# Who issues the stores of the block sums in the first mixing stage: SyncE one step later, or GpSimd right behind its additions

## The chip, the core and the metric

The kernel runs on one core of a Trainium2 chip. The core has a matrix engine (TensorE, PE in the profile) and three engines for elementwise work: VectorE (DVE), ScalarE (ACT) and GpSimd (POOL). SyncE (SP) does no arithmetic in this kernel; it issues most of the DMA transfers. ScalarE and GpSimd issue a few. Each engine takes its instructions in the order in which the program lists them, and waits on semaphores for the others.

The metric is the device time of one execution in microseconds (us). Before the change the median of three runs is 1366.9 us (1365.86 to 1368.06).

## What is computed

Two layers of the same form follow each other on 2048 tokens of width 512, all in float32. Each layer is a linear-attention block and then a gated MLP whose gate mixes the tokens:

```python
x = x + A(layernorm(x))                                   # linear attention, 32 heads
def B(x):                                                 # gated MLP with token mixing
    z  = gelu(x @ w_in)                                   # 2048 x 1792
    z1, z2 = z[:, :896], layernorm(z[:, 896:])
    g  = w_sp @ z2 + b_sp[:, None]                        # w_sp is 2048 x 2048: the mixing
    return (z1 * g) @ w_out
x = x + B(layernorm(x))
```

`w_sp` and the other weights are the same in both layers.

## The kernel before

**Precision.** A float32 product is made of three matmuls: each operand is split into a high part (ScalarE, a copy to float32r) and the remainder (VectorE, a subtraction), and high times high, high times low and low times high are added in the accumulators. In the mixing stage these three are lines 1619, 1620 and 1621.

**The mixing.** The product `w_sp @ z2` is taken with a block algorithm of Strassen's kind, which needs sums of blocks of `w_sp` as operands. The four sums of a block column are made once, in layer one, by class `Sums`, written to the DRAM tensors `s[m, k]` (m from 1 to 4, k from 0 to 7), and read back as operands in both layers. Class `P4` is the mixing. In layer one its order is eight steps each of the products P4, P1, P6, P7, P5 and P3, and then fourteen steps of a nested product N2: steps 0 to 61. A step of P4, P1 or P5 has 24 matmuls, one of P6, P7 or P3 has 18, and one of N2 has 12.

**One step `g` of `P4.run`**, in program order: `prepare(g + 2, g + 3)` splits the weights of step g + 2 (ScalarE line 1457, VectorE line 1466) and the activations of step g + 3 (ScalarE line 1462; VectorE line 1470 or 1472); `mm(g)` issues the matmuls; `fetch(g + 4)` has SyncE load the raw weights of step g + 4 into a `qd` tile (line 1413 from `w_sp`, line 1415 from the sums `s`, 512 KB each), which waits until TensorE has released such a tile; `sums.tick(g, MIX_TICKS)` is the place of the change; then come the steps of `own` (an `Inner` object, which makes the operands of N2: loads on line 1263, ScalarE and VectorE work on lines 135, 138 and 1299 to 1306, stores on line 1267), and `gates` (GpSimd lines 1639 and 1641, from step 24 on). Behind the last step of a product `evac` has VectorE add the accumulators to the result; behind P6 that is line 1669, and P7 goes on in the same accumulators, so its first matmul into each of them waits for that read.

**The sums.** `MIX_TICKS` lists the 26 steps on which block sums are made: 2, 4, 5, 7, 8, 10, 12, 14, 16 and 17 make three sums each (m = 1, 3 and 2, in this order), and the sixteen from step 20 to step 41 make one each (m = 4). SyncE loads the blocks one step ahead (`fetch`, line 1195 for the first kind, line 131 for the second), GpSimd adds (line 1209), and line 1202 stores each sum of 128 x 512 (256 KB). That is 10 x 3 + 16 = 46 stores. Another 18 are made earlier, in the token stage, by `P2.run`, which calls `sums.store()` and `sums.sum()` itself. P6 uses the sums with m = 2: its last step, 23, reads the sums that step 17 makes for k = 7, and their load is issued by `fetch(23)` in step 19.

**Pages.** Buffers of 128 x 512 are named `pg` and come from a list of 23. A page that is given back can be handed out again after six more requests (`lag=STORE`); whoever gets it waits until its last readers are done, a store's landing among them.

Of the kernel before, what the change touches and what calls it, by code (L numbers as in the profile page):

```python
# [90 lines left out]
def mixer_kernel(ctx: ExitStack, tc: tile.TileContext, x_in, wqkv, wo_d, win1_d, win2_d, wsp_d, bsp_d, wout_d,  # L91
                 ident_d, mask_d, out_d):
    nc = tc.nc
# [109 lines left out]
    class Make:  # L203
# [22 lines left out]
        def store(self, g):  # L226
            m = 2 * len(self.raw[g])
            h, l, p = self.part.pop(g)
            for n, t in enumerate((h, l)):
                nc.sync.dma_start(kept[:, m:m + 2, g, n, :], t.rearrange("p (m f) -> p m f", m=2))  # L230
            pages.put(p, l, lag=STORE)
# [942 lines left out]
    class Sums:  # L1174
# [21 lines left out]
                    raw.append(t)  # L1196
                self.raw.append(raw)

        def store(self):

            for m, k, j, t, done in self.made:
                nc.sync.dma_start(self.s[m, k][:, j, :], t)
                for t in (t, *done):
                    if id(t) in pages.held:
                        pages.put(t, lag=STORE)
            self.made = []
# [4 lines left out]

        def tick(self, i, at):

            self.store()
            if i + 1 in at:
                self.fetch()
            self.sum(i, at)

        def sum(self, i, at):

            if i not in at:
                return
            k, j, fourth = self.todo.popleft()
            if fourth:
                s2, a12 = self.raw.popleft()
                self.add(4, k, j, a12, s2, a12, s2)
            else:
                a21, a22, a11 = self.raw.popleft()
                self.add(1, k, j, a22, a21, a22)
                self.add(3, k, j, a21, a21, a11)  # L1230
                self.add(2, k, j, a11, a22, a11)
# [687 lines left out]
```

## Time and profile before

| | |
|---|---|
| median of three runs | 1366.9 us (1365.86 to 1368.06) |
| the profiled execution | 1367.67 us, of which 1366.0 us lie between the first and the last instruction |
| TensorE | busy 1355.8 us, 99% of the span |
| VectorE | busy 1030.4 us (75%) |
| ScalarE | busy 638.2 us (47%) |
| GpSimd | busy 475.8 us (35%) |
| mean granted TensorE clock | 0.997 |

The profile is one execution. In its rows a DMA issue stands under the engine that issues it, with a q for the queue (SPq, POOLq), and its length is the issue alone; the transfer lands later. `qd<-s` is a load of block sums into a quad, `s<-pg` the store of a sum from a page, `bg` the result of the mixing. A row "xN" merges N equal instructions that follow each other. The mixing stage of layer one lies between 344.6 us and some 615 us.

### The profile page before, as it was taken

The page shows a single profiled execution, that of the slowest core. Times are in us where ns is not written, and L with a number is a line of the kernel's source. Part 1 is how long each engine was busy: PE and PEld are TensorE (multiplying, and loading weights), DVE is VectorE, ACT ScalarE, POOL GpSimd, SP SyncE. Part 2 cuts the span into 40 slices and gives each one's busy share as a digit, 9 for nine tenths or more (in the row PEclk, how much of TensorE's full clock was granted, in tenths as well). Part 3 has the DMA queues.
Part 4 walks back from the last instruction along what each step waited for, and adds up shares of the span by engine and source line. Part 5 has one row for each costly group of instructions (what it writes and reads, how often), then busy time and mean ns, then how long its engine had stood idle before and what let it go on. Part 6 is the DMA issues. An engine that isn't in the chain of part 4 may idle for free.

```text
span 1366.0 us, 18322 instructions
## 1 busy us (share of the span) xinstructions
PE 1355.8 (99%) x6087; PEld 1134.7 (83%) x6087; DVE 1030.4 (75%) x1582; ACT 638.2 (47%) x1021; POOL 475.8 (35%) x551
## 2 busy tenths in 40 slices
PE   9999999999999899999999999999999999999998
PEld 7888888888888788888888888888888888888887
DVE  7985898876856788986678768887767798978642
ACT  6875553445443343442456655444455534533310
POOL 2333475533254237426421133533230011412340
PEclk9999999999999999999999999999999999999999
DMA  5762488966798888795786534666568798569652
GB/s 185 240 207 88 123 262 260 311 224 189 227 338 307 286 268 284 276 374 184 222 261 195 193 95 123 201 210 205 187 200 283 220 338 322 189 200 311 222 183 90
DMA packets 184496, 310.18 MB, mean 227 GB/s; under 512 B 15696, under 2 KB 67920, under 8 KB 180304
## 3 DMA queue, kind: packets, MB, share of 16 engines
q1 hardware_dynamic: 172736, 262.73, 58.3%
q0 software_dynamic: 8064, 39.85, 8.2%
q10 hardware_dynamic: 3600, 6.42, 1.3%
q8 instruction: 48, 0.79, 0.2%
q14 instruction: 48, 0.39, 0.1%
HBM read 211.68 MB, written 97.26 MB: 226 GB/s over the span
## 4 chain that ended last, share of the span: by engine, by line
PE 94%; DVE 3%; ACT 1%; issue 1%; DMA 1%; POOL 0%; DVEq 0%; ACTq 0%; POOLq 0%
PE bank L151 17%; PE bank L149 17%; PE bank L150 17%; PE bank L1619 9%; PE bank L1620 9%; PE bank L1621 9%; PE bank L1552 4%; PE bank L1553 4%; PE bank L1550 4%; PE bank L994 1%; PE bank L995 1%; PE bank L993 1%; PE bank L736 1%; DMA qd<-s 1%; DVE pg L138 0%
## 5 line engine op out<-in xcount | busy, mean ns | idle before, releaser
L1619 PE MATMUL bank<-qd,pg 128*128 128x512 f32 x544 | 213.1, 392 | 3.6 <-DVE bg L1669 3.6
L1620 PE MATMUL bank<-qd,pg 128*128 128x512 f32 x544 | 213.0, 392 | 0.0
L1621 PE MATMUL bank<-qd,pg 128*128 128x512 f32 x544 | 212.8, 391 | 0.0
L1466 DVE TENSOR_TENSOR qd<-qd,qd 128x1024 fp32r<-128x1024 f32 x104 | 144.2, 1387 | 78.0 <-ACT qd L1457 77.5
L1457 ACT ACTIVATE qd<-qd 128x1024 fp32r<-128x1024 f32 x104 | 110.0, 1058 | 144.6 <-DMA qd<-s 53.3
L151 PE MATMUL bank<-qd,pg 128*128 128x512 f32 x380 | 148.7, 391 | 0.3 <-DVE pg L138 0.3
L135 ACT ACTIVATE pg<-pg 128x512 fp32r<-128x512 f32 (+1 forms) x146 | 89.3, 620 | 117.4 <-DVE pg L330 43.8
L268 POOL TENSOR_SCALAR rs<-mv 128x1 f32<-128x1 f32 x95 | 42.2, 444 | 264.8 <-DVE mv L266 260.3
L1641 POOL TENSOR_TENSOR bg<-bg,pg 128x512 f32<-128x512 f32 x56 | 93.0, 1672 | 104.7 <-DMA pg<-z 93.2
L1209 POOL TENSOR_TENSOR pg<-pg,pg 128x512 f32<-128x512 f32 x52 | 81.8, 1574 | 133.3 <-DMA pg<-in_wsp_dram 121.2
L1619 PEld LDWEIGHTS bank<-qd,pg 128*128 128x128 f32 x544 | 102.8, 189 | 25.4 <-ACT qd L1457 4.0
L1620 PEld LDWEIGHTS bank<-qd,pg 128*128 128x128 f32 x544 | 102.9, 189 | 21.4
L1621 PEld LDWEIGHTS bank<-qd,pg 128*128 128x128 f32 x544 | 102.9, 189 | 21.4
L138 DVE TENSOR_TENSOR pg<-pg,pg 128x512 fp32r<-128x512 f32 (+1 forms) x143 | 107.4, 751 | 14.8 <-ACT pg L135 14.0
L149 PE MATMUL bank<-qd,pg 128*128 128x512 f32 x284 | 111.0, 391 | 0.0
L150 PE MATMUL bank<-qd,pg 128*128 128x512 f32 x284 | 110.7, 390 | 0.0
L149 PE MATMUL bank<-bg,qd 128*128 128x448 f32 x256 | 94.1, 368 | 0.0
L150 PE MATMUL bank<-bg,qd 128*128 128x448 f32 x256 | 93.7, 366 | 0.0
L330 DVE STREAM_TRANSPOSE pg<-pg 128x512 f32<-128x512 f32 x79 | 86.1, 1090 | 10.0 <-DMA pg<-yt 8.4
L151 PE MATMUL bank<-bg,qd 128*128 128x448 f32 x256 | 93.5, 365 | 0.0
L1552 PE MATMUL bank<-qd,pg 128*128 128x512 f32 x224 | 87.4, 390 | 0.3 <-DVE qd L1466 0.3
L1550 PE MATMUL bank<-qd,pg 128*128 128x512 f32 x224 | 87.2, 389 | 0.0
(220 smaller groups left out, 3192.4 us busy)
## 6 DMA issues: line engine op xcount, KB each, us to landing
qd<-s SPq DMA_DIRECT2D x64, 512.0 KB, 4.2
qd<-n POOLq DMA_DIRECT2D x32, 1024.0 KB, 7.8
pg<-in_wsp_dram SPq DMA_DIRECT2D x93, 256.0 KB, 4.7
qd<-in_wsp_dram SPq DMA_DIRECT2D x40, 512.0 KB, 5.2
s<-pg SPq DMA_DIRECT2D x58, 256.0 KB, 4.9
pg<-z SPq DMA_DIRECT2D x56, 256.0 KB, 3.9
n<-pg SPq DMA_DIRECT2D x55, 256.0 KB, 4.5
x<-pg SPq DMA_DIRECT2D x48, 256.0 KB, 2.7
```

The lines of the kernel that those rows point to most:

```text
L138: nc.vector.tensor_sub(l, src, h.bitcast(F32))
L149: nc.tensor.matmul(out, ah, bh, start=start, stop=False)
L150: nc.tensor.matmul(out, ah, bl, start=False, stop=False)
L151: nc.tensor.matmul(out, al, bh, start=False, stop=stop)
L1457: nc.scalar.activation(wh, r, AF.Copy)
L1466: nc.vector.tensor_sub(wl, r, wh.bitcast(F32))
L1550: m(out[i], h[:, o, f], w[:, o, 0], start=first and name in ("P1", "P2", "P5"), stop=False, skip_group_check=True)
L1552: m(out[i], h[:, o, f], w[:, o, 1], start=False, stop=False, skip_group_check=True)
L1619: m(out, h[:, o], w[:, 0, j, :], start=start, stop=False, skip_group_check=True)
L1620: m(out, h[:, o], w[:, 1, j, :], start=False, stop=False, skip_group_check=True)
L1621: m(out, l[:, o], w[:, 0, j, :], start=False, stop=stop, skip_group_check=True)
L1641: nc.gpsimd.tensor_tensor(u, u, z1, op=OP.mult)
```

## The change

The stores of the mixing stage are issued on GpSimd's queue instead of SyncE's. `tick` calls `store` at its end, behind this step's additions, where it called it at its beginning, for the additions of the step before. The pages are therefore also given back earlier in program order. The stores of the token stage stay on SyncE, a step later.

```diff
-        def store(self):
+        def store(self, issue=nc.sync):
 
             for m, k, j, t, done in self.made:
-                nc.sync.dma_start(self.s[m, k][:, j, :], t)
+                issue.dma_start(self.s[m, k][:, j, :], t)
                 for t in (t, *done):
                     if id(t) in pages.held:
                         pages.put(t, lag=STORE)
...
         def tick(self, i, at):
 
-            self.store()
             if i + 1 in at:
                 self.fetch()
             self.sum(i, at)
+            self.store(nc.gpsimd)
```

In the program that results, GpSimd has 46 more DMA issues, each group of three behind its three additions, and SyncE has 46 fewer. The arithmetic instructions of every engine are the same and in the same order.

## Prediction

> **What bounds the kernel now.** I read the page first, for the engine that fills the span and the groups with idle time before them.
>
> ```profile
> span 1366.0 us, 18322 instructions
> PE 1355.8 (99%) x6087; PEld 1134.7 (83%) x6087; DVE 1030.4 (75%) x1582; ACT 638.2 (47%) x1021; POOL 475.8 (35%) x551
> L1619 PE MATMUL bank<-qd,pg 128*128 128x512 f32 x544 | 213.1, 392 | 3.6 <-DVE bg L1669 3.6
> ```
>
> TensorE is busy for 99% of the span, so only its gaps can be won. The largest that the mixing shows is one of 3.6 us, ended by VectorE's line 1669, the read of the accumulators behind P6. The timeline of TensorE there:
>
> ```profile
> 431.67 0.39 PE L1619 MATMUL bank<-qd,pg 128*128 128x512 f32 x1
> ...
> 464.08 0.39 PE L1621 MATMUL bank<-qd,pg 128*128 128x512 f32 x1
> 468.06 0.76 PE L1619 MATMUL bank<-qd,pg 128*128 128x512 f32 x1 [3.59 <-DVE bg L1669]
> ...
> 475.10 0.39 PE L1619 MATMUL bank<-qd,pg 128*128 128x512 f32 x1
> ```
>
> The first row opens step 16 (P6 begins), the second is the last matmul of step 23, the third opens step 24, the last opens step 25. Eight steps of 18 matmuls run at one start per 0.227 us: (464.08 - 431.67) / 143. Step 24 should open at 464.31 and opens at 468.06: 3.75 us late. It should last 18 x 0.227 = 4.08 us and lasts 475.10 - 468.06 = 7.04: another 2.96 us. The table by windows says why (columns: TensorE, its weight loads, VectorE, ScalarE, GpSimd busy, granted clock, DMA share, GB/s):
>
> ```profile
> 460.00:465.00 5.00, 4.47 (x20) 3.38 (x18) 3.74 (x5) 1.87 (x4) 2.15 (x1) 1.00 0.81 262
> 465.00:470.00 5.00, 1.94 (x5) 1.58 (x6) 4.97 (x8) 1.33 (x2) 1.21 (x1) 0.74 1.02 321
> 470.00:475.00 5.00, 5.00 (x15) 3.92 (x14) 4.82 (x7) 1.99 (x3) 1.46 (x2) 0.58 0.97 353
> ```
>
> The granted clock is 1.00 before the gap, 0.74 and 0.58 behind it. The place costs 3.75 + 2.96 = 6.71 us, 0.49% of the span. The chain of waits leads back from it:
>
> ```profile
> 451.71 6.86 DMA qd<-s
> 458.68 1.07 ACT qd L1457
> ...
> 467.23 0.70 DVE bg L1669
> 468.06 0.76 PE bank L1619
> ```
>
> VectorE reaches line 1669 at 467.23 because a load of block sums, issued by SyncE at 451.71, landed only at 458.57, and the splits of that load and of what followed it stand ahead of line 1669 in VectorE's order: 467.23 - 458.57 = 8.66 us. Why was the load late? The timeline of SyncE and its waits between 344 and 475 us:
>
> ```profile
> 415.55 0.73 SPq L1415 DMA_DIRECT2D qd<-s  x1
> 420.59 1.58 SPq L1195 DMA_DIRECT2D pg<-in_wsp_dram  x3
> 422.28 4.47 SPq L1415 DMA_DIRECT2D qd<-s  x2
> 428.00 3.41 SPq L1202 DMA_DIRECT2D s<-pg  x3
> 431.46 1.39 SPq L1195 DMA_DIRECT2D pg<-in_wsp_dram  x3
> 432.96 0.36 SPq L1415 DMA_DIRECT2D qd<-s  x1
> 433.43 2.94 SPq L1195 DMA_DIRECT2D pg<-in_wsp_dram  x3
> ...
> 443.83 3.92 SPq L1202 DMA_DIRECT2D s<-pg  x3
> 450.34 0.32 SPq L1415 DMA_DIRECT2D qd<-s  x1
> ```
>
> ```profile
> SPq L1202 <- POOL pg L1209: 38.7, 27, 4.7
> SPq L1415 <- DMA s<-pg: 2.5, 1, 2.5
> ```
>
> Waiting at its stores (line 1202) for GpSimd's additions is by far SyncE's longest wait here, 38.7 us in 27 waits, and every load stands behind it. In the last rows of the timeline it issues the three stores of step 17 as the additions end, until 447.75; then the weights of step 23, which are one of those very sums, wait 2.5 us for the store to land, until 450.34; the load of the chain follows at 451.71.
>
> **The change part by part.** *SyncE loses 46 stores.* An issue is short (the merged 38.7 us are waiting), so what counts is the loads that move up, and they are still held by TensorE, which frees their tiles. The loads for step 16's sums stood behind step 14's stores, at 431.46; now they follow the weight load that ends at 422.28 + 4.47 = 426.75, 4.7 us sooner. Those for step 17 stood at 433.43; the weight load ahead of them waits for step 15's end, 431.67, so they go out at 432.1, 1.3 us sooner.
>
> *GpSimd gains 46 issues.* No store on its queue is in this trace; the nearest rows are its loads. The first pair is 256 KB each, the second 1 MB.
>
> ```profile
> L975 POOL DMA_DIRECT2D pg<-win_sums x24: 535/557/765, 310.3 to 1013.5; - x24
> DMA to landing us min/median/max: 3.0/4.4/6.8
> ...
> L1403 POOL DMA_DIRECT2D qd<-n x32: 527/528/596, 580.3 to 1267.7; - x32
> DMA to landing us min/median/max: 5.1/7.8/11.4
> ```
>
> An issue is 0.557 us of GpSimd's time (0.53 to 0.77), in all 46 x 0.557 = 25.6 us. What is queued behind them is the next additions, from step 24 on the gates, and from 580.3 us N2's weight loads (line 1403). The first are covered by GpSimd's own idle time:
>
> ```profile
> 426.44 4.62 POOL L1209 TENSOR_TENSOR pg<-pg,pg 128x512 f32<-128x512 f32 x3 [6.25 <-DMA pg<-in_wsp_dram]
> 436.87 10.54 POOL L1209 TENSOR_TENSOR pg<-pg,pg 128x512 f32<-128x512 f32 x6 [5.81 <-DVE qd L1466]
> ```
>
> It idles 6.25 and 5.81 us before these groups; three issues take 1.67 us. Only steps 16 and 17 follow each other without a pause (six additions in 10.54 us). If the cover is gone, their 1.67 us delay the sums of step 17, and that is in the sum below.
>
> *The path.* Step 16's additions began 436.87 - 431.46 = 5.4 us behind the first of their loads; now 426.8 + 5.4 = 432.2, and 4.62 us for three ends them at 436.8, their stores at 438.5. Step 17's loads, out at 432.1, are there at 437.5 by the same 5.4, so its additions run from 438.5 to 443.1. Their last store, m = 2, is the one that step 23 needs: it stands behind two others and starts at 443.1 + 1.1 = 444.2. Its landing takes 3.0 to 11.4 us by the rows; I take 4.4, the median for this size, so 448.6. Step 23's load can leave then instead of at 450.34: 1.7 us sooner, with bounds of 3.1 sooner (447.2) and 5.3 later (455.6).
>
> The Trainium skill prices this leg too: its page DMA: Bandwidth & Descriptors, section Anatomy of one DMA, fits 2.0 us plus bytes over 436e3 for the software path, which for 256 KB is an estimate of 2.6 us, so a landing at 446.8, 3.5 us sooner than now, and a gap of 0.2 us; the rows of this trace, 3.0 at the least, do not reach that figure.
>
> *A new wait.* The pages of step 17's loads are now those that step 14's stores release on GpSimd's queue, and SyncE would stand at them. Step 14's loads move up from 420.59 to 416.3, behind the row at 415.55, its additions began 426.44 - 420.59 = 5.85 us behind them and take 4.62, so they end at 426.8, and the third store lands at 426.8 + 1.1 + 4.4 = 432.3: 0.2 us behind the 432.1 at which SyncE wants the page. I cost it at nothing, since GpSimd is busy with step 16 until 438.5.
>
> *The sum.* With everything from step 23's load on 1.7 us sooner, line 1669 starts at 465.5 and the gap is 3.75 - 1.7 = 2.05 us. Its other end is zero: the load of the chain took 6.86 us to land, and the median of its kind is 4.2.
>
> ```profile
> qd<-s SPq DMA_DIRECT2D x64, 512.0 KB, 4.2
> ```
>
> At that latency another 2.7 us go, and VectorE is in time. The 2.96 us at the low clock came behind a gap of 3.59 us; whether a gap of 2.05 brings them no row here shows. The bounds are that they stay (gain 1.7) or go (4.66); I take that they go, as the gap is little over half as long. So the gain is 4.66 to 6.71, I take the middle, 5.7, and 1367.67 - 5.7 = 1362.0 for the profiled execution, which lies 0.77 above the median of the runs: 1361.2 for the median.
>
> The page TensorE: Matmul & The Clock Gate, Part 1 (The HAM clock gate), says that the clock halves after an idle window of about 3.4 us. The drop behind 3.59 us agrees; by that rule 2.05 us would leave the clock alone and the gain is at least 4.66, and by a rule under which any gap drops it, 1.7.
>
> What is late next? Step 25's weights, issued at 453.70 before (its tile is free at the start of step 21, 452.07), so again 1.6 us sooner; from step 26 on the fetches have caught up with TensorE. Behind step 24 I see no gap that this would open.
>
> **The rivals.** *No gain:* the last store lands as late as the 6.8 us of the longest 256 KB row, at 451.0, 0.7 us later than now, or the gap shrinks but keeps the low clock. This gives 1366.9 + 0.7 = 1367.6 to 1366.9 - 1.7 = 1365.2. For it: two stores now stand ahead of the one that matters, where SyncE had issued them while GpSimd was still adding. Against it: step 16's loads win 4.7 us.
>
> *Slower:* the software queue is the bound. The last store of step 17 lands only after the 11.4 us of that queue's longest row, at 455.6. Step 23's load then leaves 5.3 us later, the gap grows from 3.75 to 9.0 us, the low clock stays: 1366.9 + 5.3 = 1372.2. It decides from a landing of 8.8 us on (444.2 + 8.8 = 453.0, 2.7 later). For it: the 1 MB loads have a median of 7.8, and GpSimd's addition stretches from 1276 to 2370 ns in the company of VectorE, so its descriptor writing might.
>
> ```profile
> L1209 POOL TENSOR_TENSOR pg<-pg,pg x52: 1276/1525/2370, 182.1 to 554.7; 128x512 f32<-128x512 f32 x52
> ```
>
> Against it: a store is a quarter of such a load, and the issues of both groups keep to 0.53 to 0.77 us. The Trainium skill's DMA page, section SWDGE vs HWDGE vs iDMA, names the mechanism: the software path writes its descriptors through SBUF, where VectorE can lock GpSimd out, and SyncE's path is immune.
>
> **How the numbers follow.** A measurement of this kernel tells about 0.2% (2.7 us) from no change. The forecast (gap shrunk or gone, clock kept: 1360.2 to 1362.2) has 0.62, no gain 0.20, slower 0.18. Faster by over 0.2% is the forecast alone, 0.62; within 0.2% 0.20; slower 0.18. The range runs from 1359.2, the full 6.71 with another 1 us for the spread of the runs, to 1368.6, the end of "no gain" with the same 1 us; left out is the slower case.
>
> **What would show it.** In the profile after, the gap before line 1619 from line 1669 should be 2 us or none and the granted clock 1.00 from 460 to 475; SyncE's wait for line 1209 should be gone; the loads for step 16's sums should go out near 427, the weights of step 23 before 450; GpSimd's line 1202 should show 46 issues of some 0.56 us with landings near 4.4. A landing over 8.8 us, a new gap behind another product, or a gap of 3.6 that stays would prove me wrong.

## The result, and the profile after

The changed kernel is slower by a little: 1368.8 us median (1365.6 to 1371.4, 21 runs) against 1365.9 (1363.1 to 1368.5, 21 runs) for the kernel before; ratio 1.0021, 95% interval 1.0013 to 1.0029. The profiled execution took 1368.05 us. The forecast was 1361.2.

The page after, the lines that answer to those of the page before:

```profile
span 1366.3 us, 18345 instructions
PE 1354.5 (99%) x6087; PEld 1133.1 (83%) x6087; DVE 1037.8 (76%) x1582; ACT 638.4 (47%) x1021; POOL 500.9 (37%) x597
L1619 PE MATMUL bank<-qd,pg 128*128 128x512 f32 x544 | 212.2, 390 | 4.8 <-DVE bg L1669 4.8
```

GpSimd took the 25 us of issues that were expected (475.8 to 500.9). But TensorE's pause before line 1619 is still there, ended by the same line 1669, and it is 4.8 us instead of 3.6. TensorE's timeline and the table by windows (columns as before):

```profile
464.20 0.39 PE L1621 MATMUL bank<-qd,pg 128*128 128x512 f32 x1
469.38 0.53 PE L1619 MATMUL bank<-qd,pg 128*128 128x512 f32 x1 [4.79 <-DVE bg L1669]
...
475.13 0.39 PE L1619 MATMUL bank<-qd,pg 128*128 128x512 f32 x1
```

```profile
465.00:470.00 5.00, 0.62 (x2) 0.59 (x3) 3.76 (x6) 2.65 (x4) 1.82 (x2) 0.96 0.88 320
470.00:475.00 5.00, 5.00 (x17) 3.94 (x17) 4.81 (x9) 1.67 (x3) 1.83 (x2) 0.69 0.90 299
```

By the arithmetic of the prediction, step 24 opens 469.38 - 464.20 - 0.23 = 4.95 us late, and lasts 475.13 - 469.38 - 4.08 = 1.67 us too long at the low clock. The place costs 6.62 us, where it cost 6.71: the gap is 1.20 us longer, and the low clock behind it costs 1.29 us less. No view ties the second to the change, so it counts as luck. The two profiled executions are accordingly nearly equal; the medians are 3 us apart.

Was SyncE freed? Its timeline and its waits from 344 to 475 us:

```profile
426.96 1.33 SPq L1195 DMA_DIRECT2D pg<-in_wsp_dram  x3
431.98 0.33 SPq L1415 DMA_DIRECT2D qd<-s  x1
433.99 1.76 SPq L1195 DMA_DIRECT2D pg<-in_wsp_dram  x3
...
436.79 12.83 SPq L1415 DMA_DIRECT2D qd<-s  x3
...
450.69 0.36 SPq L1415 DMA_DIRECT2D qd<-s  x1
```

```profile
SPq L1415 <- DMA s<-pg: 8.7, 1, 8.7
SPq L131 <- DMA s<-pg: 5.3, 1, 5.3
```

The wait of 38.7 us at line 1202 is gone, the loads for step 16's sums go out at 426.96, and the load of the chain, step 24's, goes out at 450.69 instead of 451.71. But one wait at line 1415 grew from 2.5 to 8.7 us: SyncE now stands at the load of step 23's weights, the last of the three merged into the row at 436.79, for the landing of the sum that step 17 makes, and issues it at 449.3. (The 5.3 us at line 131 end with a load at 467.09, too late to bear on this pause.)

What holds line 1669, then? The chain of waits leads elsewhere than before:

```profile
445.73 3.45 DMA s<-pg
...
450.21 5.18 DMA pg<-in_wsp_dram
...
455.56 1.60 POOL pg L1209
...
457.45 6.99 DMA s<-pg
...
464.48 0.04 issue
464.52 0.04 ACTq L135
464.56 0.05 issue
464.60 0.04 ACT pg L135
...
465.14 1.05 ACT qd L1457
...
468.55 0.69 DVE bg L1669
```

ScalarE's line 135 (a split for `Inner`, in step 22) wants a page, and the page is still being read by the store of step 20's sum, which GpSimd issued at 457.45 and which landed 6.99 us later. The split of step 25's weights (line 1457) stands behind line 135 on ScalarE, VectorE's subtraction behind that, and line 1669 behind both. Further back the chain leads to the same landing at which SyncE stood: the blocks of step 20's sum are loaded behind step 23's weights (450.21), so the sum is added at 455.56 and stored at 457.45. The view of line 1202 names everyone who waited for such a store (its landings are those of all 64 stores of that line; the 46 on GpSimd's queue alone landed in 2.7, 5.7 and 8.0 us):

```profile
L1202 POOL DMA_DIRECT2D s<-pg x46: 539/557/583, 361.0 to 555.2; - x46
...
who waited for it (us, times):
  ACT pg L135: 5.9, 1
...
DMA to landing us min/median/max: 2.7/5.6/8.0
```

In the profile before, the same instruction of line 135 waited for VectorE only, and began at 463.28 (ScalarE's waits from 440 to 470 us, and the chain of waits); here it began at 464.60, though step 24's weights had come earlier:

```profile
ACT pg L135 <- DVE pg L1306: 3.1, 1, 3.1
```

```profile
463.28 0.40 ACT pg L135
```

The pages are given back where `store` is called. With the call at the end of the tick, each page is back a step earlier in program order, and so it is handed out to another user: line 135 drew a page that a store was still reading.

### The profile page after: what moved, and what is told of

It is laid out like the page before. It is cut to its first block, busy times and chain, and to the rows that moved or that the text cites. A ratio compares the mean times of both kernels' runs of the same rounds, so it can differ in the third digit from the quotient of the medians.

```text
span 1366.3 us, 18345 instructions
## 1 busy us (share of the span) xinstructions
PE 1354.5 (99%) x6087; PEld 1133.1 (83%) x6087; DVE 1037.8 (76%) x1582; ACT 638.4 (47%) x1021; POOL 500.9 (37%) x597
## 4 chain that ended last, share of the span: by engine, by line
PE 87%; DVE 4%; DMA 3%; ACT 2%; POOL 2%; issue 1%; SPq 0%; DVEq 0%; POOLq 0%; ACTq 0%
PE bank L151 16%; PE bank L149 16%; PE bank L150 16%; PE bank L1619 8%; PE bank L1620 8%; PE bank L1621 8%; PE bank L1552 4%; PE bank L1553 4%; PE bank L1550 4%; PE bank L995 1%; PE bank L994 1%; PE bank L993 1%; DMA s<-pg 1%; POOL pg L1209 1%; DMA pg<-in_wsp_dram 1%
## 5 line engine op out<-in xcount | busy, mean ns | idle before, releaser
L1621 PE MATMUL bank<-qd,pg 128*128 128x512 f32 x544 | 212.3, 390 | 0.0
L138 DVE TENSOR_TENSOR pg<-pg,pg 128x512 fp32r<-128x512 f32 (+1 forms) x143 | 110.6, 774 | 15.0 <-ACT pg L135 13.8
L1209 POOL TENSOR_TENSOR pg<-pg,pg 128x512 f32<-128x512 f32 x52 | 85.2, 1639 | 100.2 <-DMA pg<-in_wsp_dram 80.4
L1621 PEld LDWEIGHTS bank<-qd,pg 128*128 128x128 f32 x544 | 102.6, 189 | 21.2
L330 DVE STREAM_TRANSPOSE pg<-pg 128x512 f32<-128x512 f32 x79 | 86.1, 1090 | 10.7 <-DMA pg<-yt 8.5
```

Source lines behind the costliest of these rows:

```text
L138: nc.vector.tensor_sub(l, src, h.bitcast(F32))
L1209: nc.gpsimd.tensor_tensor(t, a, b, op=OP.add)
L1621: m(out, l[:, o], w[:, 0, j, :], start=False, stop=stop, skip_group_check=True)
```

## The experiments

The runs form three groups, each timed on one chip beside the kernel before: the first four; the reverse with the sixteen changed and the three with earlier sums; and the three runs that stand between these. The theories at first: theory 1, the pages (line 135 draws a page that a store is still reading); theory 2, the queue (stores on GpSimd cost something by themselves); a third, the place (the earlier call costs on either queue). Those of the later runs are named in their expectations. In kernels with two more lines, L1417, L1621 and L1671 are the lines 1415, 1619 and 1669 of the others.

**GpSimd's queue alone, at the old place.** The pages are handed out as in the kernel before.

```diff
         def tick(self, i, at):
 
-            self.store()
+            self.store(nc.gpsimd)
```

> The stores go out on GpSimd's queue, but at the old place, at the beginning of the next step, so that every page goes to the same holder as before the change. Theory 1 (pages): the changed kernel loses because the store at the end of the step gives its page back earlier in program order, and ScalarE's line 135 of step 22 takes that page and waits for the landing of step 20's store at 464.44 us. Then line 135 starts near 461.5 here, right behind line 1306, line 1669 follows 3.95 us later as in the kernel before, near 465.4, the gap before step 24 is 2 us or none and the clock stays at 1.00: about 1361 to 1363 us, a ratio to the kernel before of about 0.998. Theory 2 (queue): stores on the software queue cost by themselves, wherever the pages go (0.56 us of GpSimd each, landings of 5.6 us in the median against 4.9): the gap of some 4 to 5 us stays, about 1368 to 1369 us, a ratio of 1.002.

Measured: 1367.9 us (11 runs) against 1365.3 (21 runs), ratio 1.0018 (1.0009 to 1.0027). Line 135 waits for no store of a sum, and the pause is shorter in the profile, though not the 2 us or none of theory 1:

```profile
PE bank L1619 <- DVE bg L1669: 2.4, 1, 2.4
```

The clock falls behind it, the time is within 0.1 us of theory 2's range, and the ratio hardly below the changed kernel's 1.0021. So the pages are not the whole cause.

**The earlier place alone, on SyncE.**

```diff
         def tick(self, i, at):
 
-            self.store()
             if i + 1 in at:
                 self.fetch()
             self.sum(i, at)
+            self.store()
```

> The stores stay on SyncE, but are issued at the end of the step behind its additions, so that the pages go to the same holders as in the changed kernel. Theory 1: ScalarE's line 135 waits for step 20's store here too, but on SyncE that store lands some 3.4 us behind its issue (459.06 to 462.45 in the kernel before), which is before line 135 could start (463.28): no loss by the page, and SyncE still waits for GpSimd at every store: within 0.1% of the kernel before. Theory 2: as the kernel before as well. A third theory, that the earlier place costs on either queue, gives 1.002.

Measured: 1379.1 us (4 runs), ratio 1.0104 (1.009 to 1.0117), which none of the three theories foresaw. SyncE now waits for the additions of its own step, and a new pause of 10.7 us opens at the start of P6 (some 431 us):

```profile
SPq L1202 <- POOL pg L1209: 59.5, 28, 6.5
```

```profile
PE bank L1619 <- DVE bg L1666: 10.7, 1, 10.7
```

The two halves of the change belong together: the earlier place needs the other queue. Since SyncE itself is later here, the run does not tell what the pages cost.

**The changed kernel with a longer lag** (twelve page requests instead of six before a page of a store is used again).

```diff
-            self.store(nc.gpsimd)
+            self.store(nc.gpsimd, 2 * STORE)
```

> The changed kernel, but a page given back by these stores is handed out again only after 12 requests and not after 6. Theory 1: line 135 of step 22 gets a page that no fresh store holds, so the gap before step 24 is 2 us or none: 1361 to 1363 us, a ratio of about 0.998, if no other instruction gets a worse page. Theory 2: 1368 to 1369 us, a ratio of 1.002.

Measured: 1369.4 us (5 runs), ratio 1.0037 (1.0024 to 1.0051). Line 135's wait for a store is gone, the pause is 3.3 us, and another of 1.1 us stands at some 546 us. The time is 0.4 us above the range of theory 2 and far from that of theory 1; but the longer lag holds back every page of the 46 stores, out of 23 pages in all, so this run does more than take away that one wait.

**Thirty stores changed, sixteen left.** The ten steps with three sums store on GpSimd at the step's end; the sixteen with one sum (from step 20 on) store on SyncE a step later.

```diff
         def tick(self, i, at):
 
+            self.store()
             if i + 1 in at:
                 self.fetch()
             self.sum(i, at)
-            self.store(nc.gpsimd)
+            if self.made and self.made[0][0] != 4:
+                self.store(nc.gpsimd)
```

> The thirty stores of the ten steps that make three sums go out on GpSimd as in the changed kernel; the sixteen of the steps that make one sum stay on SyncE a step later, as before the change. Theory 1: the store of step 20, whose page line 135 waited for, is among the sixteen, so the wait is gone: gap of 2 us or none, 1361 to 1363 us, a ratio of about 0.998. Theory 2: thirty of 46 stores still cost, a ratio of 1.001.

Measured: 1365.0 us (11 runs), ratio 0.9996 (0.9988 to 1.0005): the loss is gone, with no gain in its place; neither forecast is met. The profile still has a pause:

```profile
PE bank L1621 <- DVE bg L1671: 2.6, 1, 2.6
```

**The reverse: sixteen changed, thirty left.** The condition reads `== 4`.

> The reverse of the run with the thirty stores of three-sum steps on GpSimd: here those thirty stay on SyncE a step later, as before, and the sixteen stores of the one-sum steps (from step 20 on) are issued by GpSimd right behind their additions, as changed. Theory S (the loss sits in the sixteen: their pages are given back one step sooner in program order, and their landings from GpSimd's queue come late): 1367.0 to 1369.5 us, with ScalarE's line 135 waiting several us for such a store's landing at some 457 to 464 us. Theory T (the loss needs the thirty as well): 1365.3 us within 0.8, gap before line 1619 about 3 us as before.

Measured: 1370.6 us (5 runs) against 1366.2 (26 runs), ratio 1.0035 (1.0022 to 1.0049), 1.1 us above the range of theory S. ScalarE's and TensorE's waits show what theory S describes (the store went out at 459.89 and landed at 466.36):

```profile
ACT pg L135 <- DMA s<-pg: 5.3, 1, 5.3
```

```profile
PE bank L1621 <- DVE bg L1671: 6.1, 1, 6.1
```

The loss sits in the sixteen stores from step 20 on, which the prediction did not look at.

**The sixteen on GpSimd's queue at the old place**, the thirty on SyncE. Against the kernel before:

```diff
-            self.store()
+            self.store(nc.gpsimd if self.made and self.made[0][0] == 4 else nc.sync)
```

> As the run with only the sixteen one-sum stores on GpSimd, but at the old place (a step later in program order), so that the pages are handed out as before; the thirty others stay on SyncE. Theory P: line 135 no longer waits for a landing of a sum's store; of the 4.4 us which the sixteen cost with the pages given back sooner, 3 us or more go: 1365.5 to 1367.5 us. Rival (the sixteen on GpSimd's queue cost it by themselves, whatever the pages): 1369 to 1371 us.

**The changed kernel and GpSimd's queue alone, once more,** beside the last run:

> The changed kernel once more, for a second profile and for its time beside the two others of this call. Theory P (the page that ScalarE's line 135 of step 22 waits for, from the store of step 20's sum): the wait at line 135 shows again with 3 to 6 us, the pause before line 1619 at some 464 us is 4 us or more, and the time is 1 us or more above the kernel with GpSimd's queue at the old place. Theory O (the second place, the end of P5 at some 542 us, where GpSimd's additions slow VectorE down): a second pause at line 1678 of 1 us or more shows too.

> All stores on GpSimd's queue, at the old place (a step later in program order, so that the pages are handed out as before), a second time, for a second profile. Theory P: no wait of line 135 for a landing of a sum's store; the time is 0.5 to 1.5 us below the changed kernel's and so 2 to 3 us above before. Where those 2 to 3 us lie is open: theory O puts them at line 1678 (some 542 us, a pause of 1 us or more); theory C (GpSimd's addition of step 21 runs beside VectorE's line 138 ahead of line 1669 and stretches it from 0.69 to 1.78 us) puts them at line 1669, with a pause of 3 us or more and the low clock behind it.

Measured, against 1365.8 us (29 runs): the changed kernel 1368.65 (12 runs), ratio 1.0019 (1.0009 to 1.003); the queue alone 1367.0 (12 runs), 1.0007 (0.9994 to 1.0021); the sixteen at the old place 1367.7 (11 runs), 1.0015 (1.0006 to 1.0025), a little above what theory P gave. In the second profile of the changed kernel the wait for the page shows again, 7.0 us, with a pause of 5.7:

```profile
ACT pg L135 <- DMA s<-pg: 7.0, 1, 7.0
```

```profile
PE bank L1619 <- DVE bg L1669: 5.7, 1, 5.7
```

The other two have no such wait. Keeping the pages as before is worth 1368.65 - 1367.0 = 1.6 us here, and, for the sixteen alone, the ratio falls from 1.0035 to 1.0015, which is 2.7 us, across two groups of runs. From the first result to the first run of the queue alone it falls by 0.4 us only (1.0021 to 1.0018). The intervals of these pairs overlap, so that the pages cost something is likely, and how much is not settled. The sixteen at the old place have a long pause without any wait for a page:

```profile
PE bank L1619 <- DVE bg L1669: 4.3, 1, 4.3
```

The pause at 542 us that theory O expected shows in none of the three profiles; theory O falls as their cause. What remains above before is 1.2 to 2.6 us, the 1.2 of this group within its noise. For it the profiles show one candidate, theory C. VectorE ahead of line 1669 with GpSimd's queue alone, and GpSimd at the same time:

```profile
463.70 0.55 DVE L1470 TENSOR_TENSOR pg<-pg,pg 128x384 fp32r<-128x384 f32 x1
464.29 1.71 DVE L138 TENSOR_TENSOR pg<-pg,pg 128x512 fp32r<-128x512 f32 x1
465.92 2.47 DVE L1669 TENSOR_TENSOR bg<-bank,pg 128x512 f32<-128x512 f32 x4
```

```profile
464.18 1.27 POOL L1209 TENSOR_TENSOR pg<-pg,pg 128x512 f32<-128x512 f32 x1 [3.51 <-PE bank L1621]
```

Line 138 takes 1.71 us beside this addition of GpSimd's, the third of the single ones and so that of step 23 (the expectation has step 21); without company it takes 0.69, and there the addition comes later. The kernel with thirty stores changed:

```profile
465.69 0.69 DVE L138 TENSOR_TENSOR pg<-pg,pg 128x512 fp32r<-128x512 f32 x1
```

```profile
466.98 1.29 POOL L1209 TENSOR_TENSOR pg<-pg,pg 128x512 f32<-128x512 f32 x1 [5.77 <-DVE bg L1671]
```

In the first run of the queue alone line 138 takes 1.78 us, and with the sixteen at the old place line 1470 takes 1.62 where it takes 0.55. That is 1.0 to 1.1 us on the path in each. It was not tried by itself: no run moved that addition and nothing else. The pause in the profiles of the queue alone is only 2.1 and 2.4 us, against the 3 that theory C asked for and the 3.6 of the kernel before, and these two executions are 1.3 and 1.7 us below the medians of their kernels. So theory C is argued, not shown, and what the 1.2 to 2.6 us hold stays open.

**Step 17's sums a step earlier.** If SyncE's long wait for that landing starts the pause, making those sums earlier ends it. The same edit on three kernels: on the one with thirty stores on GpSimd, on the kernel before, and on the changed kernel.

```diff
-MIX_TICKS = (2, 4, 5, 7, 8, 10, 12, 14, 16, 17, 20, ...
+MIX_TICKS = (2, 4, 5, 7, 8, 10, 12, 13, 15, 16, 20, ...
```

> Thirty stores on GpSimd at the step's end, sixteen on SyncE a step later, and the last three of the three-sum steps one step earlier (13, 15 and 16 in place of 14, 16 and 17). Theory B (the pause between P6 and P7 starts with SyncE standing at the load of step 23, for the landing of step 17's third sum, with the loads of steps 24 and 25 queued behind it): that load goes out at about 444.3 instead of 449.25, step 24's at about 448.4 instead of 450.6 and lands at 454 to 455; VectorE's line 1669 comes 8.6 us behind that, at 463 to 464 instead of 466.3; pause under 0.5 us, no low clock: 1359.5 to 1361.5 us. Rival Q (other waits of the stage, such as pages for line 135 or VectorE's order, set line 1669 anyway): pause of 2 us or more and 1364 to 1366 us.

> The kernel before with the last three of the three-sum steps one step earlier (13, 15 and 16 in place of 14, 16 and 17); all stores on SyncE a step later. Theory B: the third sum of step 16 is added by about 442, its store lands at 445, step 23's load goes out at about 445 instead of 450.3 and step 24's at 448.4 instead of 451.7; pause under 1 us: 1359.5 to 1362 us. Rival Q: 1364 to 1366 us. Rival V (SyncE stands longer at the stores, and the loads of step 15's and 16's blocks go out no sooner): 1365 to 1370 us.

> The changed kernel with the last three of the three-sum steps one step earlier (13, 15 and 16 in place of 14, 16 and 17). Theory B with pages: the blocks of step 20's sum are loaded some 4 us sooner, its store on GpSimd lands before 461, line 135 no longer waits for that page, and the pause goes: 1359.5 to 1362 us, within 1 us of the two other kernels with that edit. Rival G (the stores on GpSimd's queue cost 2.5 to 3.5 us by themselves, whatever the place): 2.5 to 3.5 us above the kernel before with the same edit. Rival Q: 1366 to 1369 us, as the changed kernel.

Measured, against 1366.2 us (26 runs):

| earlier sums on | median, us | ratio (95%) |
|---|---|---|
| thirty on GpSimd, sixteen on SyncE | 1361.9 (10 runs) | 0.9971 (0.9962 to 0.998) |
| the kernel before | 1363.3 (11 runs) | 0.9987 (0.9978 to 0.9995) |
| the changed kernel | 1363.4 (11 runs) | 0.9985 (0.9974 to 0.9997) |

In all three profiles the pause between P6 and P7 is gone, as theory B says and rival Q does not; the times lie 0.4 to 1.4 us above theory B's ranges. Rival G falls for this order of the sums: the changed kernel is level with the kernel before once both have the edit. The first kernel of the table beats both the kernel before and the changed one. Its windows, and SyncE's timeline:

```profile
460.00:465.00 5.00, 5.00 (x24) 4.14 (x23) 4.16 (x7) 2.79 (x4) 0.34 (x1) 1.00 0.91 289
465.00:470.00 5.00, 5.00 (x24) 4.14 (x23) 4.82 (x8) 1.61 (x3) 1.38 (x2) 1.00 1.04 384
470.00:475.00 5.00, 5.00 (x24) 4.14 (x23) 3.77 (x5) 2.22 (x4) 0.97 (x1) 1.00 1.06 391
```

```profile
436.55 11.50 SPq L1417 DMA_DIRECT2D qd<-s  x3
...
449.10 0.37 SPq L1417 DMA_DIRECT2D qd<-s  x1
```

TensorE is busy throughout these windows at full clock, and no pause shows between 340 and 620 us. The sizes were off: step 23's load, the last of the three in the first row, went out at 447.7, not 444.3, because SyncE still waits 6.6 us for the sum's landing; step 24's went out at 449.1 and landed at 454.9, line 1669 came 8.7 us behind, at 463.6, just in time. The profiles of the two others each have a pause elsewhere, at 433 us in the kernel before with this edit and at 543 us in the changed kernel with it. No run removed them; each is longer than the 1.4 or 1.5 us by which these kernels lie above the first:

```profile
PE bank L1619 <- DVE bg L1666: 1.9, 1, 1.9
PE bank L1619 <- DVE bg L1678: 2.0, 1, 2.0
```

On the changed kernel the wait for the page has gone too, since step 20's store is issued at 455.47 and lands at 458.59, before line 135 wants the page at 459.4.

## Why the prediction was wrong, point by point

- *SyncE loses its stores:* right. The wait at line 1202 is gone; step 16's loads went out at 426.96, predicted 426.8.
- *GpSimd's issues:* right at 0.557 us each, and covered as said.
- *The path to step 23's load:* right in kind, a little short. Step 17's loads waited until 434.0 to 435.4 (predicted 432.1), since the stores of step 14 were issued 1.8 us later than reckoned and landed in 5.3 to 5.7 us, not 4.4. That SyncE waits there was rightly put at nothing, since GpSimd was busy until 439.6; its additions of steps 16 and 17 took 5.1 us for three instead of 4.62. The last store of step 17 was issued at 445.73 (predicted 444.2) and landed 3.45 us later, at 449.18 (predicted 448.6), so step 23's load gained 1.0 us instead of 1.7. The Trainium skill's estimate for this leg (DMA: Bandwidth & Descriptors, Anatomy of one DMA), 2.6 us, is below every one of the 46 landings of this trace, 2.7 at the least and 5.7 in the median.
- *A new wait:* this step failed. It followed the pages that the stores give back into SyncE's loads only, and put the wait at nothing. The same pages are handed to every engine: ScalarE's line 135 in step 22 drew the one of step 20's store and waited 5.9 us for it, on the very chain to line 1669. Line 135 stood on that chain before, at 463.28, inside the 8.66 us that the prediction took as fixed between the landing of step 24's weights and line 1669; they became 11.9 (the weights landed 6.0 us behind 450.69, at 456.7). The landings were sized for step 17's store alone; the one that decided, 6.99 us, was step 20's. Of the 46 stores, the sixteen single ones got no line in the prediction, and the run with those alone carries the whole loss. How much of that loss is this wait, and how much comes with GpSimd's queue, stays open.
- *The sum:* line 1669 forecast at 465.5, measured at 468.55. The gap was to be 2.05 us or none, and is 4.95. With the queue alone, where line 135 waits for no store, line 1669 starts at 466.3 and 465.9 behind pauses of 2.4 and 2.06 us, so up to the new wait the sum was nearly right; its other end, none, needed a landing of 4.2 us for step 24's weights, and it took 6.0. *The low clock goes:* it stayed, at 1.67 us for 2.96. This step failed too: behind the 2.4 and 2.06 us of the queue alone the clock fell all the same, so a gap of 2.05 was not safe, as below.
- *The base:* the sum started from an execution at 1367.67 us, 0.77 above the median of three runs; the median of 21 runs beside the changed kernel is 1365.9, so that execution was 1.8 above it. The 6.71 us of this one place were thus more than a typical run has to give: the kernel with thirty stores moved and the earlier sums, whose profile has no pause here, lies 1366.2 - 1361.9 = 4.3 below the kernel before. In the group with the repeated changed kernel, 13 of the 29 runs of the kernel before list a mean granted clock of 1.000 (1363.0 to 1365.2 us), and 2 of 12 of the changed one.
- *The rivals:* "slower" had the sign and the kind of cause, late landings from GpSimd's queue, but placed it at step 17's store and let it decide from 8.8 us on. The store at that place landed in 3.45 us.
- *Behind step 24:* no further gap in either profile of the changed kernel, as said.

## What to carry to other kernels

Moving a store also moves the point at which its buffers are given back, so follow each buffer to its next user on every engine, not only to the queue that was to be relieved. Ask where a pause starts before making its middle shorter: here the landing of one late sum set it. Making that sum a step earlier brought 0.1% on the kernel before (ratio 0.9987) and 0.3% with thirty stores moved (0.9971), where moving all the stores alone lost 0.2%. Before summing against one profiled execution, look where it lies among the runs.

## What the runs showed of the hardware that was not expected

A pause of some 2 us is enough for the low clock, sometimes. TensorE's windows of the queue alone, second run, behind a pause of 2.06 us, and of the changed kernel's second run, behind 5.73:

```profile
465.00:470.00 5.00, 3.26 (x10) 2.58 (x11) 5.00 (x8) 0.00 (x0) 2.07 (x3) 0.77 0.99 344
470.00:475.00 5.00, 5.00 (x21) 4.12 (x20) 4.81 (x7) 2.00 (x3) 0.76 (x2) 0.89 0.90 302
```

```profile
465.00:470.00 5.00, 0.00 (x0) 0.00 (x0) 2.67 (x4) 3.04 (x4) 1.03 (x2) 0.98 0.78 290
470.00:475.00 5.00, 4.54 (x11) 3.62 (x12) 5.00 (x9) 0.59 (x2) 1.82 (x2) 0.50 0.88 272
475.00:480.00 5.00, 5.00 (x20) 4.04 (x19) 3.60 (x6) 2.99 (x5) 0.00 (x0) 0.84 0.40 126
```

Each window is 5 us. One window stands at 0.50, with its matmuls 0.43 us apart instead of 0.23, so the low clock is taken as half, and a lost share counts twice; so the time at half clock is 10 x (0.23 + 0.11) = 3.4 us in the first, and 10 x (0.02 + 0.50 + 0.16) = 6.8 us in the second; the rows of the kernel before give 10 x (0.26 + 0.42) = 6.8 us behind 3.59. So the half clock comes in pieces of some 3.4 us, each worth 1.7 us of work. How many come does not follow the length of the pause: by the same sum, pauses of 2.4, 2.6, 4.3 (the sixteen at the old place) and 4.8 us (the changed kernel's first profile) brought 3.4 to 3.5 us, pauses of 3.3 (the longer lag) and 6.1 us (sixteen changed) 6.8. Behind a pause of 1.98 us (the changed kernel with the earlier sums, 543 us) the clock fell as well, behind one of 1.95 us (the kernel before with them, 433 us) it stayed at 1.00. The Trainium skill's page TensorE: Matmul & The Clock Gate, Part 1, has the clock fall after an idle window of about 3.4 us, and says that this window runs freely. The length of the pieces agrees; that a pause must reach 3.4 us does not, since 1.98 and 2.06 were enough.
